# Combination weights by 32x32 block transposes and token combination on four row tiles, in a retention and soft-MoE kernel

## The chip, the cores and the metric

The kernel runs on one core of a Trainium2 chip. The metric is the device time of one execution in microseconds: 169.44 us for the kernel before (median of 3 runs, 169.43 to 170.0). One further execution was profiled. The engines are PE (TensorE, matrix products; PEld is its loading of weights), DVE (VectorE), ACT (ScalarE), POOL (GpSimd) and SP (SyncE, which here issues every DMA). Matrix products are written to PSUM, eight banks of 128 partitions x 512 fp32; everything else lies in SBUF.

## The reference

First a retention layer (linear attention with a decaying state) for 4 batches, 8 heads, 768 steps, head size 64; its output, 3072 tokens x 512, is the input of a soft mixture of experts with 8 experts of 4 slots each (32 slots) and 1024 hidden units.

```python
for t in range(S):
    state = gamma * state + k[:, :, t] (outer) v[:, :, t]
    y[:, :, t] = scale * q[:, :, t] @ state
x = y.transpose(0, 2, 1, 3).reshape(3072, 512)

logits = x @ phi                                   # 3072 x 32
d = exp(logits - logits.max(0)); d /= d.sum(0) + 1e-9     # softmax over the tokens
slot_input = (d.T @ x).reshape(8, 4, 512)
for e in range(8):
    slot_out[e] = maximum(slot_input[e] @ w1[e], 0) @ w2[e]
c = exp(logits - logits.max(1)); c /= c.sum(1) + 1e-9     # softmax over the slots
return c @ slot_out                                # 3072 x 512
```

All is fp32. `c`, the combination weights, and the last product are what the change is about.

## The kernel before, in words

**Retention.** The tokens go in 24 steps of 128 (`NSTEP`; 6 chunks in each of 4 batches). A step i is made of `scores` (L182: K times Q per head, two heads at once on two row tiles of 64; L187: causal mask on DVE), `attend` (L202: the state's part, L207: the scores' part, L213: scaling on DVE), `state` (L226, L228), `natural` (L234: PE transposes of y, L235: copy) and, every fourth step, the logits of a group of four steps (L245). `load_kq` and `load_vk` fetch the operands two steps ahead; v is scaled on POOL (L169) as soon as it has landed. `scores(i + 1)` is issued ahead of `natural(i)`.

**Groups.** The logits of a group g lie in a PSUM tile `ltp`, with row 32j+s for slot s of step j and a column for each of the 128 tokens of a step. `logits` takes the running maximum over tokens and the exponential for the dispatch (L256 to L272) and copies the raw logits to SBUF as `lt` (L273, on ACT). `dispatch_p` and `dispatch_u` add up d.T @ x one step later. `combine_weights`, another step later, transposes `lt` on PE (L303), so that tokens are on partitions and the slots of one token side by side, and does the softmax over the slots (L305 to L313; the last multiplication on POOL) into `cnat`. For the last group, the copy (L431) and `combine_weights` come after the dispatch has been merged.

**Splits and transposes of the weights.** `split_c(q)` takes 8 steps of `cnat` and writes, on DVE, a high part in fp32r and the rest (L322, L323), twice each; `transpose_c` brings 32 rows of weights back to partitions by PE transposes (L331), and `copy_c` (L334, on ACT) copies them to SBUF as `c4T`. Two of three are split in the last retention steps, the third after `hidden(0, 2)`; their transposes stand between the merge of the dispatch and the hidden stage's matmuls.

**Experts.** `hidden(g, k)` multiplies the slot inputs by w1, four experts at once on four column tiles of 32 (L445), for two groups of four experts and four slices of 128 inputs; `hidden_t` transposes the result on PE (L459) and clips it into a block layout (L463). The second layer (L537) goes over three blocks of output columns, `BLOCKS` = 256, 128 and 128 wide; a block takes 16 column steps (2 groups x 8 slices `fc`), each of four matmuls on four column tiles, into one bank `op`.

**Combination.** `finish(cb, op)` is a generator which is advanced once after every column step of the next block, so that its instructions are mixed into that block's. It copies `op` to SBUF (`os_`, L500), waits `Y1` column steps, replicates and adds up by a product with `rep` (L504), writes a high part and, on the lower 64 partitions, the rest as `s4` in fp32r (L506, L507), and after `Y2` more steps multiplies it by `c4T`: one fp32r matmul for 128 outputs x 512 tokens (L519). The four groups of 32 rows hold the products high x high, high x low, low x high and low x low, so that one pass adds them all. There are 24 such matmuls, three between pauses of three column steps (`BURST`). The result is copied in halves by DVE (L525) and ACT (L522) to a ring slot of 128 x 1024, and stored (L523): 12 stores of 512 KB.

**Order and memory.** PE's instructions run in the order in which the source issues them (`ORDERED`); a planner orders those of the other engines, and each engine works in that order. SP issues loads and stores in one queue. The ring (`slot`, `NRING` = 48) holds tiles of 128 x 1024 fp32 for loads of k, q, v, w1 and w2 as well as for scores, results, splits and stores; a load waits until the slot it gets is free. `load_weights` fetches w1 (L139) and w2 (L143) through all stages, in 64 loads of 512 KB.

Of the kernel before, what the change touches and what calls it, by code (L numbers as in the profile page):

```python
# [9 lines left out]
F32 = mybir.dt.float32  # L10
F32R = mybir.dt.float32r
AF = mybir.ActivationFunctionType
# [19 lines left out]
WDT = F32  # L32
BURST = (3, 3, 3)
TAIL = (2, 2, 1, 2)
# [3 lines left out]
BLOCKS = [(0, 256), (256, 128), (384, 128)]  # L38
NRING = 48
FPS = {256: 4, 192: 4, 128: 8, 64: 8}  # L40
# [37 lines left out]
def retention_soft_moe_kernel(  # L78
# [15 lines left out]
    ring = ctx.enter_context(tc.tile_pool(name="ring", bufs=NRING))  # L94
    ps = ctx.enter_context(tc.tile_pool(name="ps", bufs=1, space=PSUM))

# [3 lines left out]
    def small(name, shape):  # L100
        return cpool.tile(shape, F32, name=name)
# [11 lines left out]
    siT = small("siT", [128, NK, NSLOT])  # L113
    cnat = small("cnat", [128, NSTEP, NSLOT])
    sst = small("sst", [128, NPAIR, D])
# [134 lines left out]
    def logits(g):  # L250
        q = gs[g]
        lt = q["ltp"]
        q["pT"] = small("pT", [128, C])
        q["lt"] = small("lts", [128, C])
        if g == NGRP - 1:
            nc.vector.tensor_reduce(nmc[:, 1:2], lt, AX.X, ALU.max, negate=True)  # L256
            nc.scalar.activation(q["pT"], lt, AF.Exp, bias=nmc[:, 1:2], scale=1.0, accum_out=zc[:, 1:2])
            return
        nm = nmc[:, 0:1] if g == NGRP - 2 else small("nm", [128, 1])
        if g == 0:  # L260
            nc.vector.tensor_reduce(mrun, lt, AX.X, ALU.max)
            nc.vector.tensor_scalar(nm, mrun, -1.0, None, ALU.mult)
        else:
            mg = small("mg", [128, 1])
            nc.vector.tensor_reduce(mg, lt, AX.X, ALU.max)
            nc.vector.tensor_scalar(nm, mg, mrun, -1.0, ALU.max, ALU.mult)
        q["z"] = zrun if g == 0 else small("z", [128, 1])
        nc.scalar.activation(q["pT"], lt, AF.Exp, bias=nm, scale=1.0, accum_out=q["z"])
        if g > 0:
            q["al"] = small("al", [128, 1])  # L270
            nc.scalar.activation(q["al"], mrun, AF.Exp, bias=nm, scale=1.0)
            nc.vector.tensor_scalar(mrun, mg, mrun, None, ALU.max)  # L272
        nc.scalar.copy(q["lt"], lt)  # L273

# [7 lines left out]
    def dispatch_u(g):  # L282
# [13 lines left out]
        else:  # L296
            nc.vector.scalar_tensor_tensor(zrun, zrun, q["al"], q["z"], ALU.mult, ALU.add)
            nc.vector.scalar_tensor_tensor(acc, acc, q["al"], u, ALU.mult, ALU.add)

    def combine_weights(g):  # L300
        q = gs[g]
        lp = ps.tile([128, GRP, NSLOT], F32, name="sm", bufs=2)
        nc.tensor.transpose(lp.rearrange("p j s -> p (j s)"), q["lt"], ident)  # L303
        m = small("cm", [128, GRP])
        nc.vector.tensor_reduce(m, lp, AX.X, ALU.max)  # L305
        dst = cnat[:, GRP * g:GRP * (g + 1), :]
        nc.vector.tensor_tensor(dst, lp, m.unsqueeze(2).broadcast_to([128, GRP, NSLOT]), ALU.subtract)
        nc.scalar.activation(dst, dst, AF.Exp)
        z = small("cz", [128, GRP])
        nc.vector.tensor_reduce(z, dst, AX.X, ALU.add)  # L310
        nc.vector.tensor_scalar(z, z, 1e-9, None, ALU.add)
        nc.vector.reciprocal(z, z)  # L312
        nc.gpsimd.tensor_tensor(dst, dst, z.unsqueeze(2).broadcast_to([128, GRP, NSLOT]), ALU.mult)  # L313


    c4s, c4T = [None] * 3, [None] * 3

    def split_c(q):
        c4s[q] = slot().rearrange("p (i r h s) -> p i r h s", r=2, h=2, s=NSLOT)
        c4r = c4s[q].bitcast(F32R)  # L320
        cq = cnat[:, 8 * q:8 * q + 8].unsqueeze(2).broadcast_to([128, 8, 2, NSLOT])
        nc.vector.tensor_copy(c4r[:, :, :, 0, :], cq)  # L322
        nc.vector.tensor_tensor(c4r[:, :, :, 1, :], cq, c4s[q][:, :, :, 0, :], ALU.subtract)  # L323
        c4T[q] = slot()

    c4p = {}

    def transpose_c(q, half, tag):
        cp = c4p[q, half] = ps.tile([128, 4, 128], F32, name=tag, bufs=2 if tag == "sm" else 1)
        for j in range(4):  # L330
            nc.tensor.transpose(cp[:, j, :], c4s[q][:, 4 * half + j].rearrange("p a b s -> p (a b s)"), ident)  # L331

    def copy_c(q, half):
        nc.scalar.copy(c4T[q].bitcast(F32R)[:, half * 512:(half + 1) * 512],  # L334
                       c4p[q, half].rearrange("p j t -> p (j t)"))

# [22 lines left out]
    for i in range(NSTEP):  # L359
# [19 lines left out]
        if i >= GRP and i % GRP == 1:  # L379
            combine_weights(gp)  # L380
        if i == NSTEP - 3:
            split_c(0)
        if i == NSTEP - 2:
            split_c(1)
        if last:
# [10 lines left out]

    transpose_c(0, 0, "S")
    nj = small("nj", [128, 2, GRP])
# [6 lines left out]
    dispatch_p(NGRP - 1)  # L405
    transpose_c(0, 1, "y0")
    wj = small("wj", [128, 2])
# [18 lines left out]
    for k in range(NK):  # L426
        nc.tensor.matmul(sp[:, k, :], gs[NGRP - 1]["u"][:, k * 128:(k + 1) * 128], wsel[:, 1, :],
                         start=False, stop=True, skip_group_check=True)
    transpose_c(1, 0, "sm")
    nc.vector.tensor_tensor(siT, sp, zi.unsqueeze(1).broadcast_to([128, NK, NSLOT]), ALU.mult)  # L430
    nc.scalar.copy(gs[NGRP - 1]["lt"], gs[NGRP - 1]["ltp"])  # L431
    copy_c(0, 0)
    copy_c(0, 1)
    copy_c(1, 0)


# [3 lines left out]
    def hidden(g, k):  # L440
        if k == 0:
            hp[g] = [ps.tile([128, 512], F32, name=n) for n in (("xp", "y1"), ("y0", "S"))[g]]
        for half in range(2):
            for j in range(4):
                nc.tensor.matmul(hp[g][half][32 * j:32 * j + 32, :], siT[:, k, :],  # L445
                                 w1t[4 * g + j, k][:, half * 512:(half + 1) * 512],
                                 start=(k == 0), stop=(k == NK - 1), skip_group_check=True,
                                 tile_position=(0, 32 * j))
        if k == NK - 1:
            hs[g] = slot()  # L450
            nc.scalar.copy(hs[g][:, 0:512], hp[g][0])
            nc.vector.tensor_copy(hs[g][:, 512:1024], hp[g][1])

    def hidden_t(g):
        for half in range(2):
            tp = ps.tile([128, 4, 128], F32, name=("xp", "y1")[half])
            for f in range(4):
# [7 lines left out]
    for k in range(NK):  # L465
# [4 lines left out]
        if k == 0:  # L470
            hT = [slot().rearrange("p (f e s) -> p f e s", e=NE, s=NSLOT) for _ in range(2)]
            for t in hT:
                nc.gpsimd.memset(t, 0.0)
        if k == 2:
            split_c(2)
    hidden(1, 0)
    transpose_c(1, 1, "sm")
    copy_c(1, 1)
    load_weights(4)
# [3 lines left out]
    hidden(1, 2)  # L483
    for half in range(2):
        transpose_c(2, half, "sm")
        copy_c(2, half)
    load_weights(4)
# [3 lines left out]

    co_tags = [("sm", 2), ("xp", 1), ("y1", 1), ("sm", 2), ("S", 1)]
    pend = []
    n_co = [0]

    def finish(cb, op):
        c0, w = BLOCKS[cb]
        os_ = small("os", [128, 256])
        s4 = slot()
        nc.vector.tensor_copy(os_[:, :w], op[:, :w])  # L500
        for _ in range(Y1[cb] - 1):
            yield
        rp = ps.tile([128, 512], F32, name="y0")
        nc.tensor.matmul(rp[:, :w], rep, os_[:, :w], start=True, stop=True)  # L504
        s4r = s4.bitcast(F32R)
        nc.vector.tensor_copy(s4r[:, :w], rp[:, :w])  # L506
        nc.vector.tensor_tensor(s4r[64:128, :w], rp[64:128, :w], s4[64:128, :w], ALU.subtract)  # L507
        for _ in range(Y2[cb] - 1):
            yield
        n = 0  # L510
        for m in range((w + 127) // 128):
            mw = min(w - 128 * m, 128)
            for q in range(3):
                ot = slot()
                for half in range(2):
                    tag, nb = co_tags[n_co[0] % len(co_tags)]
                    n_co[0] += 1
                    cp = ps.tile([128, 512], F32, name=tag, bufs=nb)
                    nc.tensor.matmul(cp[0:mw], s4r[:, m * 128:m * 128 + mw],  # L519
                                     c4T[q].bitcast(F32R)[:, half * 512:(half + 1) * 512], start=True, stop=True)  # L520
                    if half:
                        nc.scalar.copy(ot[0:mw, 512:1024], cp[0:mw])  # L522
                        nc.sync.dma_start(out[c0 + m * 128:c0 + m * 128 + mw, q * 1024:(q + 1) * 1024], ot[0:mw])  # L523
                    else:
                        nc.vector.tensor_copy(ot[0:mw, 0:512], cp[0:mw])  # L525
                    n += 1
                    if n % BURST[cb] == 0:
                        for _ in range(BURST[cb]):
                            yield

    for cb, (c0, w) in enumerate(BLOCKS):
        op = ps.tile([128, 512], F32, name=("sc0", "sc1")[cb % 2])
        for g in range(2):
# [66 lines left out]
```

## Time and profile before

| | before |
|---|---|
| median of 3 runs | 169.44 us |
| profiled execution, its own time | 170.2 us |
| span of the profile (first to last instruction) | 168.4 us |
| PE busy | 153.6 us, 91% |
| DVE busy | 93.6 us, 56% |
| ACT busy | 42.0 us, 25% |
| POOL busy | 30.5 us, 18% |
| read from HBM, written to it | 57.96 MB, 6.29 MB |
| rate over the span | 381 GB/s |
| DMA queue of SP | 97.4% of 16 engines' span |

Times inside the profile count from the first instruction. The profiled execution took 1.8 us more than its span and 0.8 us more than the median of the runs. In a row of the timeline stand the start, the length, the engine, the line, the operation, the tiles (written <- read), the shape (partitions x elements) and the number of instructions; in the chain of waits, the start, the length, the engine, the tile and the line. A matmul in fp32 is two instructions, so that a row counts twice as many as the source has. "PE y L445 x8" is four matmuls. For DMA issues the profile gives the time from issue to landing, that is until all 16 parts of the transfer have been reported.

### The profile page before, as it was taken

The numbers are of one execution on the slowest core, as the hardware profiler recorded it, in microseconds if no ns is written. First come the engines' busy times: TensorE is split into PE (matmuls) and PEld (weight loads), VectorE is DVE, ScalarE is ACT, GpSimd is POOL, SyncE is SP. The second block draws the span as 40 slices with busy tenths as digits, with TensorE's granted clock in tenths as the row PEclk, the third lists the DMA queues.
The fourth block names the chain that finished last, engine by engine and source line by source line (L and its number), as shares of the span: only waits on it lengthen the run. The fifth ranks groups of instructions, "written<-read, shape, count | busy, mean of one in ns | idle before, by whom it ended". The sixth has DMA issues, their size and how long they took to land.

```text
span 168.4 us, 5648 instructions
## 1 busy us (share of the span) xinstructions
PE 153.6 (91%) x2370; PEld 109.6 (65%) x2370; DVE 93.6 (56%) x299; ACT 42.0 (25%) x104; POOL 30.5 (18%) x40
## 2 busy tenths in 40 slices
PE   8699779999999999999989799999999999999940
PEld 2577667687868786888678578867432546666620
DVE  0576445596677876694777566984223121355550
ACT  3022213232423141323212232315202030043330
POOL 0252222230304122232223221300050000000000
PEclk9999999999999999999999999999999999999998
DMA  6999999999999999999999999999999999969966
GB/s 185 324 416 411 408 402 415 401 410 406 410 407 406 407 409 406 408 409 404 407 407 411 405 409 406 403 384 367 378 312 404 415 412 406 412 263 397 384 266 263
DMA packets 18458, 64.62 MB, mean 384 GB/s; under 512 B 2048, under 2 KB 2432, under 8 KB 18432
## 3 DMA queue, kind: packets, MB, share of 16 engines
q1 hardware_dynamic: 18432, 64.26, 97.4%
q8 instruction: 19, 0.31, 0.8%
q14 instruction: 7, 0.06, 0.1%
HBM read 57.96 MB, written 6.29 MB: 381 GB/s over the span
## 4 chain that ended last, share of the span: by engine, by line
PE 50%; DMA 40%; DVE 3%; SPq 2%; issue 1%; DVEq 0%
DMA r<-in_kq_dram 18%; DMA r<-in_w_dram 18%; PE sc L537 9%; PE sc L182 6%; PE y L445 4%; PE y L207 4%; DMA r<-in_vk_dram 4%; PE xp L234 3%; PE sm L245 3%; PE y L202 3%; PE xp L445 2%; PE S L445 2%; PE sm L287 2%; PE S L226 2%; PE sm L519 2%; PE sm L331 1%
## 5 line engine op out<-in xcount | busy, mean ns | idle before, releaser
L187 DVE TENSOR_TENSOR r<-sc,kt 128x256 f32<-128x256 f32 x94 | 33.3, 417 | 17.1 <-PE sc L182 16.1
L169 POOL TENSOR_TENSOR r<-r,kt 128x512 f32<-128x512 f32 x24 | 25.1, 1044 | 75.5 <-DMA r<-in_vk_dram 51.1
L213 DVE SCALAR_TENSOR_TENSOR r<-y,kt,ysc 128x128 f32<-128x128 f32 x96 | 27.7, 343 | 9.6 <-PE y L207 6.7
L182 PE MATMUL sc<-r 64*128 64x128 f32 x376 | 27.4, 284 | 4.4 <-DMA r<-in_kq_dram 4.1
L207 PE MATMUL y<-r 128*64 128x128 f32 x384 | 27.3, 280 | 2.6 <-POOL r L169 2.4
L182 PEld LDWEIGHTS sc<-r 64*128 64x128 f32 x376 | 23.1, 187 | 7.3 <-issue 4.0
L207 PEld LDWEIGHTS y<-r 128*64 128x64 f32 x384 | 21.3, 136 | 7.3 <-POOL r L169 3.8
L235 ACT COPY r<-xp 128x512 f32<-128x512 f32 x23 | 13.5, 586 | 42.9 <-PE xp L234 33.3
L234 PE MATMUL xp<-kt,r 128*128 128x128 f32 x96 | 16.5, 287 | 0.1
L537 PE MATMUL sc<-r 128*32 128x128 f32 (+1 forms) x384 | 15.9, 310 | 0.0
L234 PEld LDWEIGHTS xp<-kt,r 128*128 128x128 f32 x96 | 10.6, 141 | 7.0 <-DVE r L187 3.4
L537 PEld LDWEIGHTS sc<-r 128*32 128x32 f32 x384 | 10.6, 110 | 6.0 <-issue 2.9
L228 ACT COPY sst<-S 128x256 f32<-128x256 f32 x20 | 7.5, 373 | 27.6 <-PE S L226 27.5
L202 PE MATMUL y<-r,sst 64*64 64x128 f32 x320 | 13.3, 282 | 0.0
L226 PE MATMUL S<-r 128*64 128x64 f32 x320 | 13.1, 222 | 0.0
L226 PEld LDWEIGHTS S<-r 128*64 128x64 f32 x320 | 12.3, 138 | 0.0
L202 PEld LDWEIGHTS y<-r,sst 64*64 64x64 f32 x320 | 8.5, 132 | 3.3 <-issue 2.1
L445 PE MATMUL y<-r,siT 128*32 128x512 f32 x64 | 8.2, 597 | 0.0
L245 PE MATMUL sm<-r,phis 128*32 128x128 f32 x192 | 7.3, 276 | 0.0
L245 PEld LDWEIGHTS sm<-r,phis 128*32 128x32 f32 x192 | 5.4, 109 | 1.4 <-issue 1.0
L313 POOL TENSOR_TENSOR cnat<-cnat,cz 128x128 f32<-128x128 f32 x6 | 2.4, 401 | 17.5 <-DVE cz L312 14.5
L287 PE MATMUL sm<-r,p 128*32 128x512 f32 x40 | 5.3, 605 | 0.0
(112 smaller groups left out, 124.2 us busy)
## 6 DMA issues: line engine op xcount, KB each, us to landing
r<-in_w_dram SPq DMA_DIRECT2D x64, 512.0 KB, 10.1
r<-in_kq_dram SPq DMA_DIRECT2D x24, 512.0 KB, 10.1
r<-in_vk_dram SPq DMA_DIRECT2D x19, 512.0 KB, 10.1
out_dram<-r SPq DMA_DIRECT2D x12, 512.0 KB, 4.3
r<-in_vk_dram SPq DMA_DIRECT2D x6, 256.0 KB, 9.6
kt<-in_consts_dram SPq DMA_DIRECT2D x1, 136.0 KB, 3.1
kt<-in_consts_dram SPq DMA_DIRECT2D x1, 78.0 KB, 5.6
phis<-in_phi_dram SPq DMA_DIRECT2D x1, 64.0 KB, 6.2
```

Source lines behind the costliest of these rows:

```text
L169: nc.gpsimd.tensor_tensor(v, v, vsc[:, i % NC, :].unsqueeze(2).broadcast_to([128, H, D]), ALU.mult)
L182: nc.tensor.matmul(sc[g // 2][r][:, g % 2, :], s["kT"][sl, g, :], s["qT"][sl, g, :], start=True, stop=True)
L187: nc.vector.tensor_tensor(A[:, r, 2 * hf:2 * hf + 2], sc[hf][r], mask.unsqueeze(1).broadcast_to([128, 2, C]), ALU.mult)
L202: nc.tensor.matmul(y[b][o:o + D, gl, :], sst[sl, g, :], s["qT"][sl, g, :], start=(gl == 0), stop=False, skip_group_check=True)
L207: nc.tensor.matmul(y[g // 2][o:o + D, g % 2, :], s["v"][:, 2 * g + r, :], s["A"][:, r, g, :], start=(c == 0 and g % 2 == 0), stop=True, sk ...
L213: nc.vector.scalar_tensor_tensor(yT[:, g, :], y[g // 2][:, g % 2, :], ybs[:, c, g:g + 1], ysc[:, g, :], ALU.mult, ALU.mult)
L226: nc.tensor.matmul(S_[r * D:(r + 1) * D, g, :], s["kn"][:, 2 * g + r, :], s["v"][:, 2 * g + r, :], start=(c == 0 and g == 0), stop=True, s ...
L234: nc.tensor.transpose(xp[:, g * 128:(g + 1) * 128], s["yT"][:, g, :], ident)
L235: (nc.vector.tensor_copy if i == NSTEP - 1 else nc.scalar.copy)(s["xn"], xp)
L245: nc.tensor.matmul(q["ltp"][32 * j:32 * j + 32, :], phis[:, p, :], st[GRP * g + j]["yT"][:, p, :], start=(p == 0), stop=(p == NPAIR - 1), ...
L445: nc.tensor.matmul(hp[g][half][32 * j:32 * j + 32, :], siT[:, k, :], w1t[4 * g + j, k][:, half * 512:(half + 1) * 512], start=(k == 0), st ...
L537: nc.tensor.matmul(op[32 * j:32 * j + 32, :w], hT[fc // 4][:, fc % 4, 4 * g + j, :], t[:, f * w:(f + 1) * w], start=(g == 0 and fc == 0), ...
```

## The change

Three things change together.

1. The logits of a group are no longer copied but block-transposed from PSUM to SBUF by one VectorE instruction (`nc.vector.transpose`, 16 blocks of 32x32 in a 128x128 tile). Within each group of 32 partitions that puts tokens on partitions and slots side by side, in four quarters of 32 tokens. `combine_weights` does its softmax there, and a second block transpose writes the weights back with slots on partitions, into `cT`: rows 32j to 32j+31 hold the weights of step j of each group. The PE transposes (L303, L331), the splits (L322, L323), the copies (L273, L334) and `cnat` are gone.
2. The combination is done as fp32 products. `rep` puts the slot outputs on all four groups of 32 partitions (`so`, one copy, no split). For half the tokens (1536) at a time, four matmuls with K = 32, one per row tile j, each multiply 128 outputs by 384 tokens (step j of three groups) and write to four different banks. DVE and ACT copy two each into an output tile `ot` of 128 x 1536, with the tokens put in order, and one DMA stores 768 KB. There are 8 such bursts, with pauses of two column steps. `ot` comes from a pool of its own with two buffers (`NOT`).
3. PSUM is divided anew when the slot inputs are done: five banks in rotation (`bank`) for the hidden stage, the transposes and the products, two for `op`, one for `rep`. The ring has 44 slots instead of 48.

```diff
-BURST = (3, 3, 3)
+BURST = (2, 2, 2)
-NRING = 48
+NRING = 44
+NOT = 2
+HALF = NTOK // 2
...
+    otp = ctx.enter_context(tc.tile_pool(name="otp", bufs=NOT))
-    cnat = small("cnat", [128, NSTEP, NSLOT])
+    cT = small("cT", [128, NGRP, C])
...
-        nc.scalar.copy(q["lt"], lt)
+        nc.vector.transpose(q["lb"].rearrange("p a s -> p (a s)"), lt)
...
     def combine_weights(g):
         q = gs[g]
-        lp = ps.tile([128, GRP, NSLOT], F32, name="sm", bufs=2)
-        nc.tensor.transpose(lp.rearrange("p j s -> p (j s)"), q["lt"], ident)
-        m = small("cm", [128, GRP])
-        nc.vector.tensor_reduce(m, lp, AX.X, ALU.max)
-        dst = cnat[:, GRP * g:GRP * (g + 1), :]
+        m = small("cm", [128, 4])
+        nc.vector.tensor_reduce(m, q["lb"], AX.X, ALU.max)
+        dst = small("cb", [128, 4, NSLOT])
...
+        nc.vector.transpose(cT[:, g, :], dst.rearrange("p a s -> p (a s)"))
...
-    transpose_c(1, 0, "sm")
     nc.vector.tensor_tensor(siT, sp, zi.unsqueeze(1).broadcast_to([128, NK, NSLOT]), ALU.mult)
-    nc.scalar.copy(gs[NGRP - 1]["lt"], gs[NGRP - 1]["ltp"])
-    copy_c(0, 0)
-    copy_c(0, 1)
-    copy_c(1, 0)
+    nc.vector.transpose(gs[NGRP - 1]["lb"].rearrange("p a s -> p (a s)"), gs[NGRP - 1]["ltp"])
+    ps_phase.__exit__(None, None, None)
+    pe = ctx.enter_context(tc.tile_pool(name="pe", bufs=1, space=PSUM, reuse_waits="tile"))
+
+    def bank():
+        return pe.tile([128, 512], F32, name="x", bufs=5)
...
-        rp = ps.tile([128, 512], F32, name="y0")
+        rp = pe.tile([128, 512], F32, name="rp")
         nc.tensor.matmul(rp[:, :w], rep, os_[:, :w], start=True, stop=True)
-        s4r = s4.bitcast(F32R)
-        nc.vector.tensor_copy(s4r[:, :w], rp[:, :w])
-        nc.vector.tensor_tensor(s4r[64:128, :w], rp[64:128, :w], s4[64:128, :w], ALU.subtract)
+        nc.vector.tensor_copy(so[:, :w], rp[:, :w])
...
         for m in range((w + 127) // 128):
             mw = min(w - 128 * m, 128)
-            for q in range(3):
-                ot = slot()
...
+            for half in range(2):
+                ot = otp.tile([128, HALF], F32, name="ot")
+                o4 = ot.rearrange("p (g j t) -> p g j t", j=GRP, t=C)
+                gr = slice(half * NGRP // 2, (half + 1) * NGRP // 2)
+                cps = [bank() for _ in range(GRP)]
+                for j in range(GRP):
+                    jp = slice(32 * j, 32 * j + 32)
+                    nc.tensor.matmul(cps[j][0:mw, 0:HALF // GRP], so[jp, m * 128:m * 128 + mw],
+                                     cT[jp, gr, :].rearrange("p g t -> p (g t)"), start=True, stop=True,
+                                     tile_position=(32 * j, 0))
+                for j in range(GRP):
+                    src = cps[j][0:mw, 0:HALF // GRP].rearrange("p (g t) -> p g t", t=C)
+                    (nc.scalar.copy if j % 2 else nc.vector.tensor_copy)(o4[0:mw, :, j, :], src)
+                nc.sync.dma_start(out[c0 + m * 128:c0 + m * 128 + mw, half * HALF:(half + 1) * HALF], ot[0:mw])
+                for _ in range(BURST[cb]):
+                    yield
```

More of the change, by code (lines that the diff above doesn't have):

```diff
@@ L10 @@
 F32 = mybir.dt.float32
-F32R = mybir.dt.float32r
 AF = mybir.ActivationFunctionType
@@ L94, in retention_soft_moe_kernel @@
     ring = ctx.enter_context(tc.tile_pool(name="ring", bufs=NRING))
-    ps = ctx.enter_context(tc.tile_pool(name="ps", bufs=1, space=PSUM))
+    ps_phase = tc.tile_pool(name="ps", bufs=1, space=PSUM)
+    ps = ps_phase.__enter__()
+    otp = ctx.enter_context(tc.tile_pool(name="otp", bufs=NOT))
     def slot():
@@ L253, in logits @@
         q["pT"] = small("pT", [128, C])
-        q["lt"] = small("lts", [128, C])
+        q["lb"] = small("lb", [128, 4, NSLOT])
         if g == NGRP - 1:
@@ L301, in combine_weights @@
         q = gs[g]
-        lp = ps.tile([128, GRP, NSLOT], F32, name="sm", bufs=2)
-        nc.tensor.transpose(lp.rearrange("p j s -> p (j s)"), q["lt"], ident)
-        m = small("cm", [128, GRP])
-        nc.vector.tensor_reduce(m, lp, AX.X, ALU.max)
-        dst = cnat[:, GRP * g:GRP * (g + 1), :]
-        nc.vector.tensor_tensor(dst, lp, m.unsqueeze(2).broadcast_to([128, GRP, NSLOT]), ALU.subtract)
+        m = small("cm", [128, 4])
+        nc.vector.tensor_reduce(m, q["lb"], AX.X, ALU.max)
+        dst = small("cb", [128, 4, NSLOT])
+        nc.vector.tensor_tensor(dst, q["lb"], m.unsqueeze(2).broadcast_to([128, 4, NSLOT]), ALU.subtract)
         nc.scalar.activation(dst, dst, AF.Exp)
-        z = small("cz", [128, GRP])
+        z = small("cz", [128, 4])
         nc.vector.tensor_reduce(z, dst, AX.X, ALU.add)
@@ L312, in combine_weights @@
         nc.vector.reciprocal(z, z)
[L313 to L335, printed above, removed]
+        nc.gpsimd.tensor_tensor(dst, dst, z.unsqueeze(2).broadcast_to([128, 4, NSLOT]), ALU.mult)
+        nc.vector.transpose(cT[:, g, :], dst.rearrange("p a s -> p (a s)"))
     load_kq(0)
@@ L380, in retention_soft_moe_kernel @@
             combine_weights(gp)
[L381 to L384, printed above, removed]
         if last:
@@ L395, in retention_soft_moe_kernel @@
             logits(i // GRP)
-    transpose_c(0, 0, "S")
     nj = small("nj", [128, 2, GRP])
@@ L405, in retention_soft_moe_kernel @@
     dispatch_p(NGRP - 1)
-    transpose_c(0, 1, "y0")
     wj = small("wj", [128, 2])
@@ L441, in hidden @@
         if k == 0:
-            hp[g] = [ps.tile([128, 512], F32, name=n) for n in (("xp", "y1"), ("y0", "S"))[g]]
+            hp[g] = [bank() for _ in range(2)]
         for half in range(2):
@@ L455, in hidden_t @@
         for half in range(2):
-            tp = ps.tile([128, 4, 128], F32, name=("xp", "y1")[half])
+            tp = bank().rearrange("p (f s) -> p f s", s=128)
             for f in range(4):
@@ L473, in retention_soft_moe_kernel @@
                 nc.gpsimd.memset(t, 0.0)
-        if k == 2:
-            split_c(2)
     hidden(1, 0)
-    transpose_c(1, 1, "sm")
-    copy_c(1, 1)
     load_weights(4)
@@ L483, in retention_soft_moe_kernel @@
     hidden(1, 2)
-    for half in range(2):
-        transpose_c(2, half, "sm")
-        copy_c(2, half)
     load_weights(4)
@@ L489, in retention_soft_moe_kernel @@
     load_weights(len(weights))
-    co_tags = [("sm", 2), ("xp", 1), ("y1", 1), ("sm", 2), ("S", 1)]
     pend = []
-    n_co = [0]
     def finish(cb, op):
@@ L498, in finish @@
         os_ = small("os", [128, 256])
-        s4 = slot()
+        so = small("so", [128, 256])
         nc.vector.tensor_copy(os_[:, :w], op[:, :w])
@@ L502, in finish @@
             yield
-        rp = ps.tile([128, 512], F32, name="y0")
+        rp = pe.tile([128, 512], F32, name="rp")
         nc.tensor.matmul(rp[:, :w], rep, os_[:, :w], start=True, stop=True)
-        s4r = s4.bitcast(F32R)
-        nc.vector.tensor_copy(s4r[:, :w], rp[:, :w])
-        nc.vector.tensor_tensor(s4r[64:128, :w], rp[64:128, :w], s4[64:128, :w], ALU.subtract)
+        nc.vector.tensor_copy(so[:, :w], rp[:, :w])
         for _ in range(Y2[cb] - 1):
             yield
-        n = 0
@@ L511, in finish @@
         for m in range((w + 127) // 128):
             mw = min(w - 128 * m, 128)
-            for q in range(3):
-                ot = slot()
[L515 to L529, printed above, removed]
+            for half in range(2):
[14 more added lines that the diff above has]
+                    yield
@@ L531, in retention_soft_moe_kernel @@
     for cb, (c0, w) in enumerate(BLOCKS):
-        op = ps.tile([128, 512], F32, name=("sc0", "sc1")[cb % 2])
+        op = pe.tile([128, 512], F32, name="op", bufs=2)
         for g in range(2):
```

## The prediction

> **What bounds the kernel now.** I read the page first, then the chain of waits from 103 us to the end, then the busy time by stretches and the DMA issues with their landings.
>
> ```profile
> span 168.4 us, 5648 instructions
> q1 hardware_dynamic: 18432, 64.26, 97.4%
> PE 50%; DMA 40%; DVE 3%; SPq 2%; issue 1%; DVEq 0%
> ```
>
> Two resources are full: the DMA queue (97.4% of 16 engines' span) and, by the chain, PE. The chain over the stretch that the change touches (start, length in us, engine, tile, line):
>
> ```profile
> 106.77 0.33 DVE r L322
> 107.30 0.40 DVE r L323
> ...
> 114.34 0.44 PE S L331 x4
> 115.07 0.44 PE y L331 x4
> ...
> 120.31 0.86 PE y L445 x8
> 121.17 0.26 PE sm L303
> 121.43 1.00 PE xp L445 x8
> ...
> 128.44 0.59 PE sm L331 x4
> 129.02 0.99 PE y L445 x8
> ...
> 133.75 1.02 PE sm L331 x8
> ...
> 138.95 6.40 PE sc L537 x128
> 145.35 0.63 PE y L504 x2
> 145.98 1.23 PE sc L537 x40
> 147.21 0.43 PE sm L519
> ...
> 159.26 0.30 DVE os L500
> 159.61 0.50 PE y L504 x2
> 160.13 0.30 DVE r L506
> 160.46 0.30 DVE r L507
> 160.90 0.48 PE sm L519
> ```
>
> From 103 to 162 us the chain is PE with a few DVE steps, and the transposes and splits that the change removes stand in it. So PE time taken out there comes off the start of the output. Whether it comes off the end is a question of the stores. The last load of w2 (L143), the last three stores (L523), and how busy the DMA engines are between them:
>
> ```profile
> L143 SPq DMA_DIRECT2D r<-in_w_dram x1: 328/328/328, 139.5 to 139.5; - x1
> DMA to landing us min/median/max: 11.0/11.0/11.0
> ```
>
> ```profile
> L523 SPq DMA_DIRECT2D out_dram<-r x3: 332/332/527, 162.2 to 163.4; - x3
> DMA to landing us min/median/max: 2.9/3.6/4.2
> ```
>
> ```profile
> core 0: us, PE busy (x) PEld busy (x) DVE busy (x) ACT busy (x) POOL busy (x), PEclk, DMA share, GB/s
> 148.00:149.50 1.50, 1.50 (x28) 1.08 (x27) 0.97 (x2) 0.63 (x2) 0.00 (x0) 1.00 0.30 109
> ```
>
> The last load lands at 139.5 + 11.0 = 150.5, though most engines have run dry at 148 (share 0.30): a DMA counts as landed when the slowest engine is through. Stores that lie behind one another land one per 1.25 us (162.2 + 2.9 = 165.1 to 163.4 + 4.2 = 167.6, two steps), so 1.88 for one of 768 KB instead of 512 KB. The shortest way of 512 KB from issue to landing is 2.9; for 768 KB I add half of that 1.25, which makes 3.53. The kernel before can have many stores in flight, since each has its own slot of the ring; its last one lands at 167.6, 0.8 before the span ends.
>
> **The change, part by part.**
>
> *Attention's end.* Away: the PE transpose L303 per group, the two splits of cnat (L322, L323; 0.73 in the chain), and a second pair of them that stands ahead of the last L213:
>
> ```profile
> 111.57 0.69 DVE L323 TENSOR_TENSOR r<-cnat,r 128x512 fp32r<-128x512 f32 x1
> 112.18 1.12 DVE L213 SCALAR_TENSOR_TENSOR r<-y,kt,ysc 128x128 f32<-128x128 f32 x4
> ```
>
> Without it L213 follows its matmuls directly, some 0.6 earlier (the DVE time from 111.57 to 112.18). With the L322/L323 steps that is 1.3, and 0.2 for the groups L331 at 114.34 and 115.07, which mostly fill PE's wait for the softmax: 1.5 in all. Added: per group two DVE block transposes of 128x128. No row shows that instruction. It can't be free, and I bound it by the DVE reduction over the same 128x128 PSUM tile (below: 281 ns) and by a 128x512 copy (687); I take 0.28, the same size. It replaces an ACT copy and lies on DVE where the splits were; the one on lb comes before L213 of the next step, whose consumer on PE stands behind other matmuls. The second one waits for POOL's multiplication, which can stand behind a wait for a vk load; with 0.4 per group (12 transposes, 3.4 in all, spread over 100 us) I cost both at nothing on the chain, and at 2 us of later output if that cover fails.
>
> *Hidden stage.* Away from PE: L303 0.26, L331 0.59 and 1.02, and after each of them the 0.14 by which the next eight L445 exceed 0.86 (1.00, 0.99): 1.87 + 0.4 = 2.3. PE being the chain here, nothing else covers these. Sum: 1.5 + 2.3 = 3.8 us. Block 0 of L537 ends now at 145.35 less three column steps (24 of the 128 instructions; four matmuls of 128 columns take 0.86 x 128/512 = 0.215, so 0.64) = 144.7; after, at 140.9.
>
> *The products.* Before, 24 fp32r matmuls of 512 columns; after, 8 bursts of four fp32 matmuls with 384 columns on four row tiles. The trace shows four column tiles at once (L445: 0.86 for 512 columns, so 0.64 for 384) and two row tiles:
>
> ```profile
> 103.96 1.16 PE L182 MATMUL sc<-r 64*128 64x128 f32 x16
> ```
>
> These are 16 instructions of 128 columns, each half of 0.215, i.e. 1.72 one after another: two do run at once. For four row tiles the bounds are 0.64 (all at once) and 2.56 a burst (none); I take 0.64, nearest to these rows, and 0.1 to 0.15 to fill and drain. By the Trainium skill (TensorE: Matmul & The Clock Gate, Part 3: Packing small matmuls — row/col tiling) four row tiles of K=32 gained 3.07 times and not 4. By that a burst takes 2.56/3.07 = 0.83 (an estimate), and the bursts on the path would end the kernel some 0.6 later; no run here shows it yet.
>
> *Evictions.* Two copies of 128x384 on each of DVE and ACT per burst:
>
> ```profile
> L525 DVE COPY r<-sm 128x512 f32<-128x512 f32 x5 | 3.4, 687 | 1.6 <-PE sm L519 1.6
> L500 DVE COPY os<-sc 128x256 f32<-128x256 f32 x1 | 0.4, 425 | 5.4 <-PE sc L537 5.4
> L522 ACT COPY r<-sm 128x512 f32<-128x512 f32 x5 | 2.8, 587 | 4.0 <-PE sm L519 4.0
> L228 ACT COPY sst<-S 128x256 f32<-128x256 f32 x10 | 3.7, 373 | 10.0 <-PE S L226 9.9
> L305 DVE TENSOR_REDUCE cm<-sm 128x4 f32<-128x128 f32 x3 | 0.8, 281 | 0.0
> ```
>
> Halfway: DVE 0.55, ACT 0.48, so 1.1 per burst. The split of s4 (L507, 0.30 in each tail) goes.
>
> *The new wait.* The copies no longer go to fresh ring slots but to `ot`, of which there are two (NOT = 2), so burst n+2 can't be copied before store n has landed. Behind that copy on DVE and ACT stand all further copies; behind them, through five banks of which a burst takes four, PE's next burst; and behind that, in PE's fixed order, the rest of L537. Worked out (us; bursts 1 to 4 belong to block 0, 5 and 6 to block 1, 7 and 8 to block 2):
>
> - `so` and five column steps after 140.9, burst 1 starts at 143.2, its store is issued at 145.2; burst 2's at 146.5. Both queue behind the loads: landed at 150.5 + 1.88 = 152.4, and 154.3.
> - Burst 3 is multiplied by 147, but copied from 152.4 on, done 153.5, store out 153.6, landed + 3.53 = 157.2.
> - Burst 4 waits for burst 3's banks (PE stands from 148 to 153): multiplied by 154.3, copied 155.4, store 155.5, landed 159.1. Two column steps end block 1 at 154.7.
> - Its `os` waits for those copies (155.7), then rep, `so` and five steps: burst 5 at 157.3, copied 159.2, landed 159.3 + 3.53 = 162.8. Burst 6: copied 160.5, landed 162.8 + 1.88 = 164.7.
> - Block 2 ends at 161.5 (before: 159.2); `os`, rep, `so`: burst 7 at 162.8, copied 164.7, landed 168.3; burst 8 waits for its third bank until 164.7, is copied at 166.0, lands at 168.3 + 1.88 = 170.2.
>
> Against 167.6 that is 2.6 us later. The 3.8 us gained ahead of it vanish in the wait for store 1, which the loads set: with nothing gained (144.7) the same steps end only 0.2 later. By the Trainium skill (DMA: Bandwidth & Descriptors, Anatomy of one DMA) a DMA has a fixed cost of some 2.0 us beside its bytes; with 1.92 for 768 KB that is 3.9 where the rows give 3.53. It speaks against few buffers: put into the same steps, the end would come some 0.4 later (an estimate).
>
> *NRING 44 for 48.* Some loads may wait for a slot near 99 us, but the slots that the splits and transposed weights held are free again, and the slowest DMA engine is 2.6 us behind the others at 150: I cost it at nothing, 1 us of later loads if not.
>
> **The rivals.**
>
> *The gain arrives (faster).* If two tiles suffice, because the first stores land before burst 3 needs them, only the queue is left: 150.5 + 8 x 1.88 = 165.5, 2.1 sooner, 167.3. For it: the idle DMA stretch at 148 to 149.5 is filled. Against it: store 1 can't pass the loads, and burst 3 is ready 5 us before 152.4. The Trainium skill (Trainium Kernel Development and Optimization, Best Practices) holds double buffering to be enough to overlap DMA with compute; that is this rival.
>
> *It cancels (same).* If the last load lands 2 us earlier, at 148.5, where most engines now end, each step moves with it: 168.2, + 0.6 us, 170.0, within or at the edge of what a measurement can tell. For it: fewer slots are taken in the hidden stage. Against it: the slowest engine seems never short of work.
>
> *Row tiles don't overlap (much slower).* 2.56 per burst instead of 0.64; in the same steps the last store lands at 176, so 178. At 1.6 per burst the same steps end at 173.9. For it: no row has four row tiles. Against it: L182.
>
> *PE slows down after its stall (slower still).* The last matmul and the clock after it:
>
> ```profile
> 162.15 0.49 PE L519 MATMUL sm<-r 128*128 128x512 f32 x1
> ```
>
> ```profile
> 167.00:167.40 0.40, 0.00 (x0) 0.00 (x0) 0.00 (x0) 0.00 (x0) 0.00 (x0) 0.92 0.04 10
> 167.40:168.40 1.00, 0.00 (x0) 0.00 (x0) 0.00 (x0) 0.00 (x0) 0.00 (x0) 0.50 0.00 0
> ```
>
> About 4.7 us after PE's last work the granted clock is halved. The stall before burst 4 is of just that length. Halved, the 0.64 + 0.43 + 0.43 + 0.3 of PE work up to the next rep come twice: + 1.8, so 173.8. By the Trainium skill (TensorE: Matmul & The Clock Gate, Part 1) the gate looks at free-running windows of 3.4 us, which a stall of 4.7 holds whole in 4 of 10 cases; the row agrees with some such length.
>
> **How the numbers follow.** The profiled execution took 170.2 for a span of 168.4; the median of the runs is 169.44. I add 2.6 to the median (the same step on the profiled execution: 172.8): 172.0. Chances: stores on two tiles set the pace, 0.52, within 170.5 to 173.2; with the slow clock, 0.12; row tiles apart, 0.04; it cancels, 0.14 (169 to 170.3); the gain arrives, 0.18. Slower by over 0.5% (what a measurement here can tell from no change) is thus 0.68, same 0.14, faster 0.18. The range is to leave out half of the faster case and the row-tile one: 168.0 to 174.2; the forecast's own is 170.5 to 173.2.
>
> **What would show it.** Right: copies of `ot` on DVE and ACT that wait some 5 us for a store near 147 to 153; PE idle then, with L537 broken; block 2 ending after 160; stores never more than two in flight. No L303/L331 and block 0 done near 141 show the first part alone. Wrong: PE busy without a break to 157, stores landing 1.9 apart from 152 on, or bursts of 2.5 us.

## The result, and the profile after

The changed kernel takes 177.34 us (median of 4 runs, 175.91 to 178.09) against 169.69 us for the kernel before: a ratio of 1.044, with a 95% interval of 1.037 to 1.051. It is slower, as forecast, but by 7.6 us and not by 2.6, and above the forecast range of 168.0 to 174.2. The profiled execution is the fastest of the four: 175.91 us, a span of 174.0. In the experiments below, runs more than 1.5% above the fastest of their kernel are left out of times and ratios, so that some times differ by 0.1 us from those that the expectations name. From its page, the span, PE, the load and store queue, and the chain by engine:

```profile
span 174.0 us, 5654 instructions
PE 157.5 (90%) x2380; PEld 111.1 (64%) x2380; DVE 93.2 (54%) x306; ACT 38.4 (22%) x96; POOL 30.7 (18%) x40
q1 hardware_dynamic: 17856, 64.26, 94.1%
DMA 54%; PE 38%; DVE 2%; SPq 2%; issue 1%; DVEq 0%; ACT 0%
```

The bytes are the same (64.26 MB), but the queue's share fell from 97.4% to 94.1%, and DMA has taken PE's place at the head of the chain. The chain of waits over the stretch that was shown of before:

```profile
118.27 10.51 PE x L421 x96
128.78 1.02 PE x L435 x8
...
142.09 0.63 PE rp L471 x2
142.72 1.23 PE op L501 x40
143.95 0.89 PE x L485 x8
144.85 1.01 DVE ot L490 x2
...
145.93 7.13 DMA out_dram<-ot
...
153.53 0.57 DVE ot L490
...
154.15 2.11 PE x L485 x6
156.25 1.87 PE op L501 x32
...
164.36 0.30 DVE os L467
...
167.20 1.39 PE x L485 x6
...
168.59 0.56 DVE ot L490
```

The hidden stage (L421, before L445) runs without the breaks that L303 and L331 made and begins at 118.27 (before 119.32); rep of block 0 stands at 142.09 (before 145.35). From the first store on, the kernel hangs on that store: 7.13 us from issue to landing, then the copies of burst 3 (L490), then the rest of burst 4 on PE. Up to there the chain is that of the prediction. Block 2 ends at 164.36 (before 159.26). The last load, the first store and the sixth:

```profile
L146 SPq DMA_DIRECT2D r<-in_w_dram x1: 328/328/328, 141.1 to 141.1; - x1
DMA to landing us min/median/max: 10.1/10.1/10.1
```

```profile
L491 SPq DMA_DIRECT2D out_dram<-ot x1: 347/347/347, 145.9 to 145.9; - x1
DMA to landing us min/median/max: 7.1/7.1/7.1
```

```profile
L491 SPq DMA_DIRECT2D out_dram<-ot x1: 332/332/332, 163.2 to 163.2; - x1
DMA to landing us min/median/max: 5.3/5.3/5.3
```

The last load has landed at 151.2, store 1 at 153.1, store 6 at 168.5. And the stall with the granted clock (the number before the DMA share):

```profile
core 0: us, PE busy (x) PEld busy (x) DVE busy (x) ACT busy (x) POOL busy (x), PEclk, DMA share, GB/s
148.80:149.70 0.90, 0.85 (x5) 0.24 (x2) 0.00 (x0) 0.00 (x0) 0.00 (x0) 1.00 1.04 428
149.70:151.20 1.50, 0.00 (x0) 0.00 (x0) 0.00 (x0) 0.00 (x0) 0.00 (x0) 0.99 1.04 433
151.20:153.10 1.90, 0.00 (x0) 0.00 (x0) 0.00 (x0) 0.00 (x0) 0.00 (x0) 0.50 0.82 343
153.10:158.00 4.90, 3.85 (x38) 2.34 (x38) 2.43 (x5) 1.76 (x4) 0.00 (x0) 0.50 0.54 214
158.00:160.00 2.00, 2.00 (x50) 1.63 (x50) 0.29 (x1) 0.00 (x0) 0.00 (x0) 1.00 0.79 316
```

PE stands from 149.7 to 154.1, its clock is halved from 151.2, and what follows the stall up to 158 runs at that clock.

### The profile page after: what moved, and what is told of

Same layout as the page of the kernel before. It is cut to its first block, busy times and chain, and to the rows that moved or that the text cites. A ratio compares the mean times of both kernels' runs of the same rounds, so it can differ in the third digit from the quotient of the medians.

```text
span 174.0 us, 5654 instructions
## 1 busy us (share of the span) xinstructions
PE 157.5 (90%) x2380; PEld 111.1 (64%) x2380; DVE 93.2 (54%) x306; ACT 38.4 (22%) x96; POOL 30.7 (18%) x40
## 3 DMA queue, kind: packets, MB, share of 16 engines
q1 hardware_dynamic: 17856, 64.26, 94.1%
## 4 chain that ended last, share of the span: by engine, by line
DMA 54%; PE 38%; DVE 2%; SPq 2%; issue 1%; DVEq 0%; ACT 0%
DMA r<-in_w_dram 23%; DMA r<-in_kq_dram 18%; DMA r<-in_vk_dram 9%; PE op L501 8%; PE x L421 8%; PE x L485 5%; DMA out_dram<-ot 4%; PE sc L185 3%; PE y L210 3%; PE xp L237 2%; PE sm L248 2%; PE y L205 1%; DVE ot L490 1%; PE x L435 1%; PE rp L471 1%
## 5 line engine op out<-in xcount | busy, mean ns | idle before, releaser
L210 PE MATMUL y<-r 128*64 128x128 f32 x384 | 30.1, 286 | 3.0 <-POOL r L172 1.9
L210 PEld LDWEIGHTS y<-r 128*64 128x64 f32 x384 | 23.4, 140 | 8.2 <-issue 4.7
L501 PE MATMUL op<-r 128*32 128x128 f32 (+1 forms) x384 | 16.8, 322 | 0.0
L485 PE MATMUL x<-cT,so 32*128 32x384 f32 x64 | 11.7, 567 | 5.0 <-DVE ot L490 4.5
L501 PEld LDWEIGHTS op<-r 128*32 128x32 f32 x384 | 11.1, 114 | 7.7 <-issue 4.9
L490 DVE COPY ot<-x 128x384 f32<-128x384 f32 x16 | 8.3, 553 | 13.3 <-DMA out_dram<-ot 6.7
L421 PE MATMUL x<-r,siT 128*32 128x512 f32 x128 | 14.1, 594 | 0.4 <-DVE siT L404 0.4
L229 PE MATMUL S<-r 128*64 128x64 f32 x320 | 14.2, 228 | 0.0
L490 ACT COPY ot<-x 128x384 f32<-128x384 f32 x16 | 7.0, 481 | 29.1 <-PE x L485 23.3
L485 PEld LDWEIGHTS x<-cT,so 32*128 32x128 f32 x64 | 4.9, 194 | 8.3 <-DVE ot L490 6.2
```

The source lines that it names most:

```text
L210: nc.tensor.matmul(y[g // 2][o:o + D, g % 2, :], s["v"][:, 2 * g + r, :], s["A"][:, r, g, :], start=(c == 0 and g % 2 == 0), stop=True, sk ...
L229: nc.tensor.matmul(S_[r * D:(r + 1) * D, g, :], s["kn"][:, 2 * g + r, :], s["v"][:, 2 * g + r, :], start=(c == 0 and g == 0), stop=True, s ...
L485: nc.tensor.matmul(cps[j][0:mw, 0:HALF // GRP], so[jp, m * 128:m * 128 + mw], cT[jp, gr, :].rearrange("p g t -> p (g t)"), start=True, sto ...
L490: (nc.scalar.copy if j % 2 else nc.vector.tensor_copy)(o4[0:mw, :, j, :], src)
L501: nc.tensor.matmul(op[32 * j:32 * j + 32, :w], hT[fc // 4][:, fc % 4, 4 * g + j, :], t[:, f * w:(f + 1) * w], start=(g == 0 and fc == 0), ...
```

## The experiments

Theory A is the prediction's: copies wait for stores, because two output tiles are too few for stores that lie behind the loads. B: the halved clock is a good part of the loss. C: the products on row tiles and the block transposes cost it. D: the ring with 44 slots delays the loads. E (too few PSUM banks for the bursts) came up with the version in ring slots. "Slots" below are those of the ring; two slots hold as much as two tiles of 512 KB, three as much as two of 768 KB. The kernel before took 169.84 to 169.86 us in the rounds of the experiments.

| kernel | output tiles | slots | us | ratio to before, 95% interval |
|---|---|---|---|---|
| changed kernel | 2 x 768 KB | 44 | 177.34 | 1.044 (1.037 to 1.051) |
| four tiles (two runs) | 4 x 768 KB | 41 | 172.93 | 1.019 (1.014 to 1.023) |
| fewer slots | 2 x 768 KB | 41 | 180.71 | 1.064 (1.059 to 1.070) |
| output in ring slots | ring, 512 KB | 47 | 169.91 | 1.000 (0.998 to 1.002) |
| the same, 44 slots | ring, 512 KB | 44 | 169.78 | 0.999 (0.998 to 1.001) |
| two small tiles | 2 x 512 KB | 45 | 178.51 | 1.049 (1.044 to 1.055) |
| four small tiles | 4 x 512 KB | 43 | 174.43 | 1.030 (1.025 to 1.034) |
| PE kept warm | 2 x 768 KB | 44 | 175.94 | 1.038 (1.031 to 1.044) |
| changed kernel, again | 2 x 768 KB | 44 | 178.42 | 1.052 (1.048 to 1.056) |
| PE kept warm, again | 2 x 768 KB | 44 | 175.98 | 1.037 (1.032 to 1.042) |
| six banks | ring, 512 KB | 47 | 168.42, 168.40 | 0.994 (0.991 to 0.998), 0.993 (0.990 to 0.995) |
| six banks, spread | ring, 512 KB | 47 | 169.22 | 0.996 (0.992 to 0.999) |

**Four tiles, and the slots they cost.**

```diff
-NRING = 44
-NOT = 2
+NRING = 41
+NOT = 4          # the control has NRING = 41 and NOT = 2
```

> The changed kernel with four output tiles instead of two (NOT = 4), and 41 ring slots instead of 44 to make room. Theory A (with two tiles, the copies of burst 3 wait for store 1, which lies behind the loads): with the matmul, copy and store times of the changed kernel's profile, the last store lands near 166.6 instead of 172.95, PE has no stall between 148 and 154 and the clock stays up; about 168.7 us. Theory C (the products on four row tiles and the block transposes are themselves the loss): no gain, 175 to 178. Theory D (the smaller ring delays the loads, and that is the loss): not better than the changed kernel, rather 1 to 2 us worse. Between A and D: 170 to 171.

> The changed kernel with 41 ring slots and still two output tiles: the control for the four tiles. A: the ring only shifts the last load, at most 1 us; 176 to 179. D: the last load lands 1 to 2 us after 151.2, and the time goes up by as much or more, 178 to 180.

At the same 41 slots, four tiles gain 7.8 us over two (180.71 to 172.93; the smaller number is the middle of only two runs). A holds, and C as the whole of the loss does not: nothing in the products differs. But 172.93 is far from the 168.7 that A alone gives, and three slots fewer cost the changed kernel 3.4 us against its first measurement (177.34 to 180.71) and 2.3 against its second (178.42). So D is there too, and I had missed both numbers by taking A for the whole. The profile of four tiles (of a run of 175.22 us) shows how the two work together: its last load lands at 154.6 and store 1 at 156.6, and the copies of burst 5, which need the first tile again, wait 4.3 us for that store.

**Ring slots instead of tiles.** Twelve bursts of 256 columns and 512 KB, each into a slot:

```diff
-            for half in range(2):
-                ot = otp.tile([128, HALF], F32, name="ot")
+            for q in range(3):
+                ot = slot()
...
-NRING = 44
+NRING = 47       # second run: 44
-BURST = (2, 2, 2)
+BURST = (1, 2, 1)
```

> The changed kernel with its output in ring slots of 1024 tokens again: 12 bursts of four matmuls of 256 columns, 12 stores of 512 KB, 47 ring slots, pauses of one or two column steps; block transposes, row tiles and the new division of PSUM stay. A: no copy waits for a store, the last store lands near 166; 167.5 to 169. C: 172 or more, with PE longer in the products than before. D: as with A, since the ring is nearly as before.

> The version with its output in ring slots (12 stores of 512 KB, run before at 169.99 us with 47 slots) with 44 slots: the ring's share alone, without a wait for output tiles. Theory D (three slots fewer bring the last load later, from 149.1 to 151 or 152, and the time goes with it): 171 to 172.5 us. Against D: 170 within 0.5.

All that the change lost is back, with its transposes, row tiles and PSUM division still in: C is out as a cause of the loss. And with stores in slots three slots fewer do not change the time, 169.91 against 169.78, though they do change the loads. The last load with 47 slots and with 44:

```profile
L145 SPq DMA_DIRECT2D r<-in_w_dram x1: 328/328/328, 138.3 to 138.3; - x1
DMA to landing us min/median/max: 10.8/10.8/10.8
```

```profile
L145 SPq DMA_DIRECT2D r<-in_w_dram x1: 328/328/328, 142.7 to 142.7; - x1
DMA to landing us min/median/max: 10.2/10.2/10.2
```

149.1 and 152.9: three slots push the last load back by 3.8 us, and the time by nothing: the stores follow it in the queue, and in neither version does a copy wait for a store. In these runs, later loads cost time only where tiles run out.

**Tiles of 512 KB in a pool.** The same version again, with tiles:

```diff
-                ot = slot()
+                ot = otp.tile([128, 1024], F32, name="ot")
...
-NRING = 47
+NRING = 45       # with NOT = 4: 43
```

> The same version with 45 ring slots and its output in a pool of two tiles of 512 KB: the wait for output tiles, at nearly the same ring. Theory A: copies of burst 3 and all later ones wait for the store two before; with 12 stores, each 2.9 us from issue to landing and 0.8 of copies, the last one lands near 173.6 instead of 167.4, about 176 us, more if PE's clock falls in the stalls. Without A: 170 to 171.

> The version with 12 stores of 512 KB, from a pool of four tiles with 43 ring slots (two tiles and 45 slots gave 178.51 us, ring slots 169.9). Theory A: with four tiles in flight a copy waits for the fourth store before, which costs little: the burst that needs tile 1 again is ready about 4.5 us after store 1 was issued, which then takes 4 to 8 us behind the loads; 170 to 172.5. If it were the pool as such or the smaller ring: 175 or more.

With two tiles, 8.6 us are lost against ring slots (169.91 to 178.51), A's 176 and more. Later loads have no part in it: in this profile, with 45 slots, the last load lands at 149.0, as with 47 slots.

```profile
L146 SPq DMA_DIRECT2D r<-in_w_dram x1: 328/328/328, 138.9 to 138.9; - x1
DMA to landing us min/median/max: 10.1/10.1/10.1
```

The copies' waits for stores in the same profile (engine, tile, line <- what ended the wait: us in total, times, longest):

```profile
ACT ot L490 <- DMA out_dram<-ot: 8.7, 3, 4.0
DVE ot L490 <- DMA out_dram<-ot: 8.5, 5, 4.2
```

In the version with ring slots the same copies wait for nothing but PE:

```profile
ACT r L489 <- PE x L484: 22.4, 12, 11.4
DVE r L489 <- PE x L484: 7.9, 12, 1.6
```

Four small tiles come to 174.43, between the two and above what I expected. In their profile, of a run of 178.47 us, the last load lands at 154.7 and a copy still waits 5.7 us for a store: with 43 slots the loads come 5.7 us later than with 45, which takes back part of what the tiles give. No run separates the two.

**PE kept warm.** Work for PE ahead of burst 4, whose result nothing reads:

```diff
+                if cb == 0 and m == 1 and half == 1:
+                    wp = pe.tile([128, 512], F32, name="rp")
+                    for _ in range(5):
+                        nc.tensor.matmul(wp, rep, cT[:, 0:4, :].rearrange("p g t -> p (g t)"), start=True, stop=True)
                 cps = [bank() for _ in range(GRP)]
```

> The changed kernel with five more matmuls of 128x512 (their result is read by nothing) right ahead of burst 4, some 4.3 us of PE work in a stall of 5.4 us. Theory B (a good part of the loss is the granted clock, halved from 151.0 to 157.8 after the stall): the clock stays at 1.00, the stall stays, and the time falls by 2 to 3.5 us, to 173.5 to 175. A without B: the store times alone decide, within 0.5 us of the changed kernel's 177.3.

The first time it took 175.94 us, ratio 1.038 (1.031 to 1.044), between what B and what A alone had led to, and with an interval that overlaps the changed kernel's. So both were run again in the same rounds:

> The changed kernel itself, on the same chip and in the same rounds as the one kept warm, since their first intervals overlap: 176 to 178.5 us.

> The changed kernel with the five extra matmuls ahead of burst 4, as before. Theory B (the halved clock is a good part of the loss): 2 us or more below the changed kernel of this call. Against B, by its profile (the last store lands at 172.55 instead of 172.95, because the stores and not PE set the pace after the stall): 0.3 to 1.5 us below it.

Now the intervals are apart: 178.42 and 175.98, so keeping PE busy is worth 2.4 us here. The clock from 152 to 160 in the changed kernel of this comparison:

```profile
152.00:154.00 2.00, 0.17 (x1) 0.00 (x0) 0.00 (x0) 0.00 (x0) 0.00 (x0) 0.81 0.92 383
154.00:156.00 2.00, 0.29 (x2) 0.29 (x4) 0.90 (x2) 0.86 (x2) 0.00 (x0) 0.50 0.19 78
156.00:158.00 2.00, 2.00 (x14) 0.91 (x16) 1.24 (x3) 0.56 (x2) 0.00 (x0) 0.50 0.36 148
158.00:160.00 2.00, 2.00 (x34) 1.53 (x26) 0.29 (x1) 0.33 (x1) 0.00 (x0) 0.50 1.03 411
```

and in the one kept warm:

```profile
152.00:154.00 2.00, 2.00 (x5) 0.69 (x5) 0.00 (x0) 0.00 (x0) 0.00 (x0) 1.00 0.67 280
154.00:156.00 2.00, 1.35 (x7) 0.59 (x6) 1.02 (x2) 0.86 (x2) 0.00 (x0) 1.00 0.07 29
156.00:158.00 2.00, 2.00 (x42) 1.14 (x39) 1.31 (x3) 0.90 (x2) 0.00 (x0) 1.00 0.65 252
158.00:160.00 2.00, 2.00 (x49) 1.31 (x48) 0.29 (x1) 0.00 (x0) 0.00 (x0) 1.00 1.03 418
```

B holds as a part: some 2 of the 8 us. The wait for the stores stays. One thing besides the stall differs, though. In this profile of the changed kernel (179.14 us) the clock is halved once more, from 119.1 to 122.5, while PE works almost without a break, and in that of the one kept warm (175.98 us) it is not:

```profile
115.70:119.00 3.30, 3.06 (x28) 2.31 (x20) 1.47 (x10) 1.08 (x5) 0.40 (x1) 1.00 0.89 339
119.10:122.40 3.30, 3.26 (x16) 0.78 (x20) 0.21 (x1) 0.00 (x0) 0.00 (x0) 0.50 1.00 379
```

The extra matmuls come long after that and can't have prevented it. Its share of the 2.4 us was not separated.

**Six banks.** With ring slots block 0 ends 2.7 us earlier than before (`os` at 142.09 instead of 144.77), and block 2 does not: its `os` stands at 159.35 (before 159.26). In the timeline every second burst is long (start, length):

```profile
146.99 0.71 PE L484 MATMUL x<-cT,so 32*128 32x256 f32 x8
147.63 0.42 PE L500 MATMUL op<-r 128*32 128x128 f32 x8
...
147.99 1.23 PE L484 MATMUL x<-cT,so 32*128 32x256 f32 x8
...
159.35 0.29 DVE L466 COPY os<-op 128x128 f32<-128x128 f32 x1 [0.53 <-PE op L500]
```

A burst needs four of five banks, so three of its matmuls wait for copies of the burst before. Theory E: this is where the gain of 2.7 us goes. The edit gives rep's bank to the rotation; the second run also starts and spaces the bursts otherwise (`Y1` = 3, 3, 2; `Y2` = 5, 6, 2; `BURST` = 2, 3, 1).

```diff
-        rp = pe.tile([128, 512], F32, name="rp")
+        rp = bank()
...
-        return pe.tile([128, 512], F32, name="x", bufs=5)
+        return pe.tile([128, 512], F32, name="x", bufs=6)
```

> The version with its output in ring slots (47), the product with rep taken from the rotation and the rotation given its bank: six banks instead of five, of which a burst takes four. Theory E (what keeps that version from being faster than the kernel before is that every second burst waits for the copies of the one before it, 1.2 us instead of 0.65 on PE): block 2 ends 1 to 2 us before 159.2, the last store lands at 165.5 to 166.5, 168 to 169 us. Against E: 170 within 0.5.

> The six banks with the bursts of block 0 started one or two column steps earlier and two steps apart, those of block 1 three steps apart. Theory E: the copies of a burst (0.84 us on DVE) are done before the next one begins, so PE loses nothing more, and the first stores start earlier; equal to the six banks or up to 1 us faster, 167.5 to 168.5.

> The version with ring slots and six banks again, with more rounds: 168 to 169 us, 0.3 to 1.0% below the kernel before.

168.42 us, and 168.40 when run again: 0.993 (0.990 to 0.995), 0.7% below the kernel before. From the second profile:

```profile
147.43 0.91 PE L484 MATMUL x<-cT,so 32*128 32x256 f32 x8
...
157.84 0.29 DVE L466 COPY os<-op 128x128 f32<-128x128 f32 x1 [0.52 <-PE op L500]
```

The long burst has shrunk from 1.23 to 0.91, and block 2 ends at 157.84 instead of 159.35. So E holds for 1.5 of the 2.7 us; where the rest goes was not traced. Spreading the bursts added nothing: 169.22 us, above the 167.5 to 168.5 that I expected, at 0.996 with an interval that overlaps the other's.

## Why the prediction was wrong, step by step

*Attention's end and the hidden stage* (3.8 us gained): 3.3 in the first profile, by rep at 142.09 and 145.35. The hidden stage gave 2.2 of its 2.3; attention's end gave 1.0 and not 1.5 (118.27 against 119.32). In the second profile of the changed kernel, with the clock halved from 119.1 to 122.5, rep stands at 144.54 and only 0.8 is left. The block transposes take what the reduction row had suggested, 0.28 forecast, 0.31 measured:

```profile
101.59 0.31 DVE L316 STREAM_TRANSPOSE cT<-cb 128x128 f32<-128x128 f32 x1 [0.58 <-POOL cb L315]
```

*The new wait*: right in place, order and sign. Store 1 landed 1.9 after the last load (1.88 forecast), PE stood from 149.7 to 154.1 (148 to 153 forecast), and the version without the wait loses nothing. That the 3.8 us gained earlier would vanish in it holds too. The size failed: the last store landed at 172.95 in the first profile, which is of the fastest run, and at 176.2 in the second (179.14 us), where 170.2 was forecast. In the first, nearly all of the 2.75 is there when block 1 ends, at 157.33 instead of 154.7. Two steps of the prediction failed:

- *"NRING 44 for 48 ... I cost it at nothing."* The last load landed at 151.2 in the first profile and at 152.8 in the second, instead of 150.5, and it goes with the number of slots: in all profiles of these versions it landed at 149.1 to 149.9 with 47 slots, 149.0 with 45, 151.2 to 152.9 with 44, 154.7 with 43, 154.6 and 156.1 with 41. So what I had named as cover, the freed slots and the slowest DMA engine, did not cover it. While the copies wait for store 1, most of such a delay is paid: from the second profile to the one with 41 slots the last load comes 3.4 us later (152.8 and 156.1) and the last store 2.8 (176.2 and 179.0). The last load in the second profile:

```profile
L146 SPq DMA_DIRECT2D r<-in_w_dram x1: 328/328/328, 141.7 to 141.7; - x1
DMA to landing us min/median/max: 11.1/11.1/11.1
```

- *The slow clock*, left out of the sum as a rival with a chance of 0.12. It came in both profiles of the changed kernel, after the stall from 151.2 to 158.0 and from 153.2 to 163.5. The price was near: 1.8 forecast, 1.4 between the first medians with and without the extra matmuls (177.34 and 175.94, from different rounds, with overlapping intervals) and 2.4 between the second. The chance rested on PE's end in the profile before, where 4.7 us passed until the clock fell, and on a window that has to be idle as a whole; after the stall began it took 1.5 us, so that this condition can't be the right one here.

In the second profile, which ends 6.0 us later than forecast, the two come to some 4.3 (an estimate: 2.8/3.4 of the 2.3 by which the last load is late, and the 2.4 between the medians). What the other runs owe to each was not traced. Two more terms were mis-sized:

- *Stores at 1.88 apart.* Stores 1 and 2 kept it; store 6 took 3.4 after store 5 (168.5 against 161.7 + 3.4 = 165.1), as one part of its 16 came last: 15 had landed by 166.9. In the first profile that costs at most some 0.5, as the last copies also need PE's burst 8, which ends at 168.59 (chain above). With PE kept warm, in the second comparison, such delays count: that chain runs through stores 2, 4 and 6, which took 8.2, 5.3 and 5.0 us from issue to landing. A store nearly alone in the queue took 3.3, which is below the 3.53 forecast, and below the 3.9 that the prediction got by the Trainium skill (DMA: Bandwidth & Descriptors, Anatomy of one DMA). That section is about DMAs issued by GpSimd; here SyncE issues them.
- *A burst at 0.64, and 0.1 to 0.15 to fill and drain.* From the first burst's start to the next instruction it takes 0.86:

```profile
143.88 0.93 PE L485 MATMUL x<-cT,so 32*128 32x384 f32 x8
144.74 0.64 PE L501 MATMUL op<-r 128*32 128x128 f32 x16
```

With 256 columns (146.99 to 147.63 in the version with ring slots, above) it takes 0.64. So 128 columns more cost 0.22, the pace of four column tiles (0.215): the four row tiles do overlap, and what the forecast had too small is a fixed part of some 0.2 per burst. Of the two prices that were set side by side, the Trainium skill's (TensorE: Matmul & The Clock Gate, Part 3: Packing small matmuls — row/col tiling), a gain of 3.07 and 0.83 a burst, is the nearer at 384 columns: 2.56/0.86 = 3.0. At 256 columns the gain is 1.72/0.64 = 2.7, so it is no fixed factor.

Of the rivals, row tiles that don't overlap at all are out, and so is the gain that arrives: two tiles were not enough. The Trainium skill (Trainium Kernel Development and Optimization, Best Practices) says "Double-buffer for performance" without naming a condition; here two buffers cost 8.6 us against ring slots, and the measurement decides.

## What to carry to other kernels

The number of output tiles has to cover the time from issue to landing as it is where the stores stand in the queue (7.1 us behind loads, 3.3 alone), not the transfer's own time. Two buffers that wait for landings can put a delay of a load, of a store's last part and of the clock on the critical path; the same output through a ring already there cost nothing here. After PE work has been taken out, look at what PE waits for next: here a rotation of five banks for bursts of four, where one bank more turned no gain into 0.7%.

## What the runs showed of the hardware that I had not expected

Four row tiles of K = 32 at once kept the pace of four column tiles per column here, with a fixed part on top: a burst of four fp32 matmuls takes 0.64 us with 256 columns and 0.86 with 384, so 0.22 for 128 columns and some 0.2 besides. The granted clock fell 1.5 us after PE's last matmul, where at the end of the kernel before it took 4.7; and once, at 119.1, it fell after 3.3 us in which PE was busy for 3.06. In these three cases neither the length of PE's pause nor its busy time foretold the fall; what counts as work was not tested. And one part of a store's 16 can land 1.6 us after the other 15, which any wait for that store pays.
